# The order of GpSimd's first load and the identity matrix in an attention and gated feed-forward kernel

## The chip, the cores and the metric

The kernel runs on one core of one Trainium2 chip. The metric is the device time of one execution in microseconds (us). Five engines work side by side in a core, each with its own queue of instructions: TensorE (PE in the profile, with PEld for its weight loads), VectorE (DVE), ScalarE (ACT), GpSimd (POOL) and SyncE (SP). DMA transfers are issued from the queues of SP, ACT and POOL, and are carried out by 16 DMA engines.

## The reference

Eight batches of eight heads are read crosswise with a small state, and the result goes through a feed-forward layer with a gate:

```python
def _attn_ref(x, state) -> np.ndarray:          # x (8, 8, 512, 64), state (8, 8, 32, 64)
    scores = scale * np.matmul(x, state.transpose(0, 1, 3, 2))
    ...
    xread = np.matmul(a, state)
    scores2 = scale * np.matmul(state, x.transpose(0, 1, 3, 2))
    ...
    sread = np.matmul(a2, x)
    return np.concatenate([xread, sread], axis=2).astype(np.float32)

def _moe_ref(x, w_gate, w_val, w_out) -> np.ndarray:   # x (4352, 512), d_ff 1536
    gate = np.maximum(x @ w_gate, 0.0)
    val = x @ w_val
    return (gate * val @ w_out).astype(np.float32)
```

The output has 4352 rows of 512 values in float32: for each batch 512 rows from x and 32 from the state.

## The kernel before

The work goes by batch. For each of the eight batches, x is brought in, converted to bf16 (tile xb) and transposed (xT); scores against the transposed state (stT) go to PSUM; ACT takes their exponential (e_sn), and DVE sums and scales it (a_sn), which is transposed once more (ans). Instead of reading the state and then multiplying by the gate and value weights, the kernel first multiplies the state by the weights (tile U, from `u_mm`, L303) and then the attention by U (`gv_mm`, L328). `relu` on ACT and `mult` on DVE make the gated hidden rows (h_sb), and `out_mms` (L365) multiplies them by the output weights. Matmuls of 512 columns at L328 and L365 are most of PE's work.

The order on every engine is written out by hand: `tc.manual_schedule()` at L410 keeps the order in which the instructions are written, and the string `program` (from L456) lists the steps of the first batches one by one, with the PSUM banks that they use. From L492 on, loops go on through the rest. Waits between engines are placed by the framework where data demand them.

What happens at the very start is what the change touches. In the order of the code:

- DVE clears a small tile, `warm` (L411), which PE multiplies by itself (`spin`, L447) while it waits for data. Such spins stand at several places of the program and run whether data are late or not.
- Three loads go out on the hardware queues (L413 to L418): the first pair of heads of batch 0 on SP; on ACT the first part of the state (`state_dma`, L98) and then the second pair of heads. Each pair is 256 KB of float32.
- `make_identity` (masks.py 197 and 199) fills the tile id128, called id in the profile: a memset and an affine select, both on GpSimd. PE uses it as the moving operand of each transpose on PE.
- ACT computes one exponential (L420), so that its table is there.
- DVE sums the identity into a 128 x 2 mask, `odd` (L421), which tells for each partition to which half it belongs. `state_conv` (L122 on ACT) multiplies the state by a column of it.
- GpSimd issues its first load (L427): heads 4 to 7 of batch 0, called the tail (`x_tail`), cast to bf16 on the way into xb, 512 KB of float32.
- The program begins. GpSimd goes on with two such loads for batch 1 (`dx`, L435) and then with the gate and value weights in slices (`dw`, L111), 14 loads in turn, and more after them.

For batch 0, PE's first steps are: the state's transposes (`state_T`, L130), those of the first two pairs of heads (`x_T`, L178), one spin, the scores of these heads (`att_sc`, L209), and then the transposes of the tail (`x_T`, L182), which need the load of L427. The tail's scores, batch 1 (L195), and the first matmuls with the weights (`c_unit`, L303) follow.

Of the kernel before, what the change touches and what calls it, by code (L numbers as in the profile page):

```python
# [12 lines left out]
AX = mybir.AxisListType  # L13
# [3 lines left out]
def kernel(  # L17
# [9 lines left out]
    nc = tc.nc  # L27
# [34 lines left out]
    id128 = const.tile([128, 128], BF16, name="id128")  # L62
# [4 lines left out]
    odd = const.tile([128, 2], FP32, name="odd")  # L67
# [92 lines left out]
    def x_tail(b):  # L160
        return xb[b][:, NC * HK * D:].rearrange("p (h c d) -> p c h d", c=NC, h=HK)
# [251 lines left out]
    for eng, j in ((nc.sync, 0), (nc.scalar, None), (nc.scalar, 1)):  # L413
        if j is None:
            state_dma(eng, 0, 2)
        else:
            src = x[0, 2 * j:2 * j + 2].rearrange("h (p c) d -> p h c d", c=NC)
            eng.dma_start(out=xf[0][:, 2 * j:2 * j + 2], in_=src)  # L418
    make_identity(nc, id128)
    nc.scalar.activation(out=tiny, in_=nc.const_aps.tensor(0.0, (128, 1), FP32), func=AF.Exp)  # L420
    nc.vector.reduce_sum(out=odd, in_=id128.rearrange("p (a h m) -> p h a m", h=2, m=8), axis=AX.XY)  # L421

    def w_load(w, lo, n):
        w_dma((moe_w_gate, moe_w_val)[w], (wg_sb, wv_sb)[w], lo, lo + n)
# [1 line left out]
    xb_alloc(0)  # L426
    nc.gpsimd.dma_start(out=x_tail(0).rearrange("p c h d -> p h c d"),  # L427
                        in_=x[0, HK:H].rearrange("h (p c) d -> p h c d", c=NC))

    def x_load(b, part, parts):  # L430
        if part == 0:
            xb_alloc(b)
            xb[b] = xb[b].rearrange("p (h c d) -> p c h d", h=H, c=NC)
        hs = slice(H * part // parts, H * (part + 1) // parts)
        nc.gpsimd.dma_start(out=xb[b][:, :, hs].rearrange("p c h d -> p h c d"),  # L435
                            in_=x[b, hs].rearrange("h (p c) d -> p h c d", c=NC))
# [154 lines left out]
```

## Time and profile before

| what | us |
|---|---|
| three runs, median (lowest to highest) | 222.43 (221.5 to 223.79) |
| span of the profiled execution, first to last instruction | 219.9 |
| median less that span | 2.5 |
| PE busy in the span | 215.0 |
| DVE busy | 130.3 |
| ACT busy | 124.0 |
| POOL busy | 49.0 |
| DMA: queue of L427, from issue to landing | 6.1 |

For the profiled execution the page gives the span alone; the times of whole executions are those of the three runs. A view of waits gives an engine, the line and tile that waited, what it waited for, and then the sum in us, the number of times and the longest. The chain that ended last is followed back from the last instruction; each of its rows has start, length and what ran. A timeline row has start, length, engine, line, operation, and the tiles written and read. A row of busy time by stretches has the stretch, its length, the busy time of PE, PEld, DVE, ACT and POOL with the number of instructions, the granted clock of PE, the share of the 16 DMA engines that was busy (it can exceed 1 where packets overlap) and GB/s. A row of a DMA queue has packets, MB and the share of the 16 engines' time.

### The profile page before, as it was taken

To read this page: it belongs to the slowest core of one execution; us is meant where nothing else is said; L and a number is where in the kernel's file an instruction comes from. 1 tells how busy PE (TensorE), PEld (TensorE's weight loads), DVE (VectorE), ACT (ScalarE), POOL (GpSimd) and SP (SyncE) were. 2 spreads that over 40 slices of the span, in tenths; PEclk is the share of its full clock that TensorE was granted. 3 is DMA by queue.
4 is the path that set the end of the run, shared out by engine and by line. 5 is a ranking of instruction groups with operands and counts; after the bars stand their busy time and mean duration, and the time that the engine had idled before them with its cause. 6 is when DMAs were issued, how large, how long until landed. Compare 5 with 4: busy or idle time off the path is not lost.

```text
span 219.9 us, 4854 instructions
## 1 busy us (share of the span) xinstructions
PE 215.0 (98%) x1947; PEld 105.1 (48%) x1947; DVE 130.3 (59%) x228; ACT 124.0 (56%) x237; POOL 49.0 (22%) x54
## 2 busy tenths in 40 slices
PE   7899999999999999999999999999999999999994
PEld 3554455444444444444444444445444445666544
DVE  2697898964787569665766487648675333322100
ACT  5599887555667557555566555646654544222222
POOL 8777845360000616015000600000000000000000
PEclk9999999999999999999999999999999999999999
DMA  7999999194048593881358116701411112111132
GB/s 152 176 194 197 197 243 271 64 177 142 22 106 244 102 284 101 136 255 49 96 122 269 52 20 145 118 15 48 105 43 54 49 48 48 52 66 67 57 98 95
DMA packets 41383, 26.27 MB, mean 119 GB/s; under 512 B 22576, under 2 KB 36784, under 8 KB 41360
## 3 DMA queue, kind: packets, MB, share of 16 engines
q1 hardware_dynamic: 28496, 17.73, 31.2%
q0 software_dynamic: 11968, 7.47, 22.1%
q10 hardware_dynamic: 896, 0.75, 1.3%
q8 instruction: 15, 0.25, 0.4%
q14 instruction: 8, 0.07, 0.1%
HBM read 18.35 MB, written 8.91 MB: 124 GB/s over the span
## 4 chain that ended last, share of the span: by engine, by line
PE 94%; DMA 4%; ACT 1%; issue 0%; POOL 0%; DVE 0%; DVEq 0%; POOLq 0%
PE o_ps L365 39%; PE gv_ps L328 38%; PE gv_ps L345 5%; PE up L303 4%; DMA xb<-in_x_dram 3%; PE sc_ps L209 2%; PE upc L303 2%; PE sr_ps L273 1%; PE xT_ps L195 1%; DMA out_dram<-o_sb 1%; PE warm_ps L447 1%; PE aT_ps L244 0%; PE xT_ps L182 0%; ACT o_sb L373 0%; ACT xT L186 0%
## 5 line engine op out<-in xcount | busy, mean ns | idle before, releaser
L365 PE MATMUL o_ps<-wo_sb,h_sb 128*128 128x512 bf16 x372 | 94.6, 379 | 0.0
L328 PE MATMUL gv_ps<-ans,U 128*128 128x512 bf16 x384 | 94.1, 379 | 0.0
L356 DVE TENSOR_TENSOR h_sb<-gv_ps,g_sb 128x512 bf16<-128x512 f32 x96 | 65.2, 689 | 44.7 <-ACT g_sb L352 43.7
L352 ACT ACTIVATE g_sb<-gv_ps 128x512 bf16<-128x512 f32 (+1 forms) x108 | 63.2, 591 | 43.4 <-PE gv_ps L328 32.0
L328 PEld LDWEIGHTS <-U 128*128 128x128 bf16 x384 | 36.3, 98 | 42.2 <-issue 0.6
L365 PEld LDWEIGHTS <-h_sb 128*128 128x128 bf16 x372 | 35.4, 98 | 41.0 <-issue 2.4
L373 ACT COPY o_sb<-o_ps 128x512 f32<-128x512 f32 x31 | 18.3, 590 | 16.5 <-PE o_ps L365 16.5
L313 DVE CAST U<-up 128x512 bf16<-128x512 f32 x36 | 22.7, 684 | 5.0 <-PE up L303 5.0
L313 ACT CAST U<-up 128x512 bf16<-128x512 f32 x36 | 18.9, 594 | 11.7 <-PE up L303 11.7
L151 POOL CAST xb<-xf 128x1024 bf16<-128x1024 f32 x10 | 10.1, 1040 | 65.6 <-DMA xf<-in_x_dram 40.4
L216 ACT ACTIVATE e_sn<-sc_ps 128x512 bf16<-128x512 f32 x16 | 9.6, 599 | 11.1 <-PE sc_ps L209 11.1
L265 POOL COPY xa<-xb 128x2048 bf16<-128x2048 bf16 (+1 forms) x9 | 15.5, 1746 | 1.2 <-POOL xb L151 0.9
L356 DVE TENSOR_TENSOR hs_sb<-gv_ps,g_sb 128x256 bf16<-128x256 f32 x12 | 5.1, 425 | 15.3 <-PE gv_ps L345 10.1
L222 DVE TENSOR_REDUCE cs<-e_sn 128x16 f32<-128x512 bf16 x16 | 10.9, 680 | 4.0 <-ACT e_sn L216 4.0
L228 DVE TENSOR_TENSOR a_sn<-e_sn,rc 128x512 bf16<-128x512 bf16 x16 | 12.6, 793 | 0.4
L323 ACT CAST U<-upc 128x512 bf16<-128x512 f32 (+1 forms) x21 | 10.1, 574 | 0.5 <-PE upc L303 0.4
L303 PEld LDWEIGHTS <-stT 64*32 64x32 bf16 x512 | 5.5, 90 | 9.0 <-issue 7.6
L209 PEld LDWEIGHTS <-xT 128*128 128x128 bf16 x128 | 5.8, 99 | 4.2 <-DVE xT L186 0.8
L303 PE MATMUL up<-wg_sb,stT 64*32 64x512 bf16 x144 | 7.5, 380 | 0.0
L303 PE MATMUL up<-wv_sb,stT 64*32 64x512 bf16 x144 | 7.2, 380 | 0.0
L345 PE MATMUL gv_ps<-br,wg_sb 128*128 128x256 bf16 x48 | 7.2, 273 | 0.0
L345 PE MATMUL gv_ps<-br,wv_sb 128*128 128x256 bf16 x48 | 7.2, 273 | 0.0
(62 smaller groups left out, 116.7 us busy)
## 6 DMA issues: line engine op xcount, KB each, us to landing
out_dram<-o_sb SPq DMA_DIRECT2D x30, 256.0 KB, 2.5
xf<-in_x_dram SPq DMA_DIRECT2D x4, 1024.0 KB, 6.5
wo_sb<-in_moe_w_out_dram POOLq DMA_DIRECT2D x2, 768.0 KB, 13.6
wg_sb<-in_moe_w_gate_dram POOLq DMA_DIRECT2D x5, 256.0 KB, 8.6
wv_sb<-in_moe_w_val_dram POOLq DMA_DIRECT2D x5, 256.0 KB, 9.2
xf<-in_x_dram POOLq DMA_DIRECT2D x1, 1024.0 KB, 15.3
xb<-in_x_dram POOLq DMA_DIRECT2D x3, 256.0 KB, 6.5
xb<-in_x_dram POOLq DMA_DIRECT2D x1, 512.0 KB, 12.0
```

The source lines that it names most:

```text
L209: nc.tensor.matmul(ps[:, :, c, jj], xT[b][:, c, 2 * jp + jj], stT[:, b, 2 * jp + jj], start=True, stop=True)
L222: nc.vector.reduce_sum(out=cs, in_=e_v, axis=AX.X)
L228: {"dve": nc.vector, "pool": nc.gpsimd}[eng].tensor_tensor(out=by_pair(a_sn[b], jp).rearrange("p r (j n) -> p r j n", n=Ns), in0=e_v, in1= ...
L265: nc.gpsimd.tensor_copy(out=v[:, hs:hs + src.shape[1]], in_=src)
L303: nc.tensor.matmul(dst[parity][32 * j:32 * j + 32], stT[r:r + 64, b, j, 32 * parity:32 * parity + 32], wsb[r:r + 64, j, lo:lo + n], start= ...
L313: copy[eng](out=U[b][:, w, kc, lo:lo + 512], in_=held["u", b, w, lo][kc])
L328: nc.tensor.matmul(ps[w], U[b][:, w, kc, f0:f0 + 128], ANS[b][:, kc].rearrange("p c t -> p (c t)"), start=(kc == 0), stop=(kc == NK - 1))
L345: nc.tensor.matmul(ps[w][:, 0:nt], wsb[:, j, f0:f0 + 128], br[:, j].rearrange("p b n -> p (b n)"), start=(j == 0), stop=(j == NJ - 1))
L352: nc.scalar.activation(out=g_sb[:, 0:n], in_=ps[0][:, 0:n], func=AF.Relu)
L356: nc.vector.tensor_tensor(out=dst, in0=ps[1][:, 0:n], in1=held["g", b, jf][:, 0:n], op=ALU.mult)
L365: nc.tensor.matmul(held["o", b, tsub], src[:, jf, tsub * 128:(tsub + 1) * 128], wo_sb[:, jf], start=(jf == 0), stop=(jf == NF - 1))
L373: copy[eng](out=o_sb, in_=held["o", b, tsub])
```

## The change

The identity and the mask are written behind the issue of GpSimd's first load instead of ahead of it. No operation is added or taken away.

```diff
             eng.dma_start(out=xf[0][:, 2 * j:2 * j + 2], in_=src)
-    make_identity(nc, id128)
     nc.scalar.activation(out=tiny, in_=nc.const_aps.tensor(0.0, (128, 1), FP32), func=AF.Exp)
-    nc.vector.reduce_sum(out=odd, in_=id128.rearrange("p (a h m) -> p h a m", h=2, m=8), axis=AX.XY)
 
     def w_load(w, lo, n):
         w_dma((moe_w_gate, moe_w_val)[w], (wg_sb, wv_sb)[w], lo, lo + n)
@@ -426,6 +424,8 @@
     xb_alloc(0)
     nc.gpsimd.dma_start(out=x_tail(0).rearrange("p c h d -> p h c d"),
                         in_=x[0, HK:H].rearrange("h (p c) d -> p h c d", c=NC))
+    make_identity(nc, id128)
+    nc.vector.reduce_sum(out=odd, in_=id128.rearrange("p (a h m) -> p h a m", h=2, m=8), axis=AX.XY)
 
     def x_load(b, part, parts):
```

On GpSimd the issue of L427 comes first, then the memset and the affine select of the identity, then the loads of the program. On DVE the sum keeps its place between the memset of L411 and the cast of the first pair of heads (L155). The queues of SP, ACT and PE have the same instructions in the same order as before.

## The prediction

> **What bounds the kernel now.** I read the page first, for the engine that is full. PE is busy for 215.0 of the 219.9 us of the span, and the granted clock (PEclk) is at 9 tenths or more in every slice.
>
> ```profile
> span 219.9 us, 4854 instructions
> PE 215.0 (98%) x1947; PEld 105.1 (48%) x1947; DVE 130.3 (59%) x228; ACT 124.0 (56%) x237; POOL 49.0 (22%) x54
> ```
>
> So a change of order at the start can only act on the few microseconds in which PE has nothing to do. The view of waits, for PE alone, has just three of them:
>
> ```profile
> PE warm_ps L447 <- DVE hs_sb L411: 1.2, 1, 1.2
> PE xT_ps L182 <- DMA xb<-in_x_dram: 0.6, 1, 0.6
> PE stT_ps L130 <- ACT st_b L122: 0.2, 1, 0.2
> ```
>
> The middle one belongs to the load that is moved. The chain that ended last, in its first 14 us, has the same load as one piece of 6.10 us, with the identity matrix in front of it:
>
> ```profile
> 0.75 0.18 POOL id masks.py:197
> 0.94 0.07 issue
> 1.00 0.29 POOL id masks.py:199
> 1.29 0.14 issue
> 1.43 6.10 DMA xb<-in_x_dram
> 7.52 0.04 issue
> 7.57 0.66 PE xT_ps L182 x16
> ```
>
> The reader is to see that on paper the change takes 0.71 us (1.43 less 0.72, when POOL starts its first own work) off the head of this chain. Then I asked whether the 6.10 us really begin with the issue. The busy time by stretches says what the 16 DMA engines do meanwhile (last two columns: DMA share, GB/s):
>
> ```profile
> 3.25:3.50 0.25, 0.25 (x2) 0.15 (x1) 0.00 (x0) 0.00 (x0) 0.25 (x1) 1.00 1.06 369
> 3.50:3.75 0.25, 0.25 (x2) 0.00 (x0) 0.00 (x0) 0.20 (x1) 0.25 (x1) 1.00 1.12 393
> 3.75:4.00 0.25, 0.25 (x2) 0.00 (x0) 0.00 (x0) 0.25 (x2) 0.25 (x2) 1.00 1.46 283
> 4.00:4.25 0.25, 0.25 (x1) 0.00 (x0) 0.23 (x1) 0.25 (x2) 0.25 (x1) 1.00 0.86 94
> ```
>
> They are full from 2.5 us on, with other loads. The DMA view, cut to short windows, gives packets, MB and share by queue. q0 (software) carries POOL's loads, q1 SP's and q10 ACT's. First 3.50 to 3.75 us, then 3.75 to 4.00, then 4.50 to 5.00:
>
> ```profile
> q10 hardware_dynamic: 94, 0.10, 109.0%
> q1 hardware_dynamic: 3, 0.00, 2.5%
> ...
> q10 hardware_dynamic: 72, 0.06, 73.5%
> q0 software_dynamic: 14, 0.01, 72.4%
> ...
> q0 software_dynamic: 132, 0.07, 130.6%
> ```
>
> The moved load, issued at 1.43, has not one packet before 3.75 us. Its packets begin as ACT's last load (the second x pair) ends: q10 has 94 packets in one quarter of a microsecond, 72 in the next, and 17 from 4.0 to 4.5. The queue of SP has run out just before. So up to about 4 us the load seems to wait for engines, not for its issue.
>
> **The change part by part.**
>
> *The issue, moved ahead.* POOL's rows before are memset 0.72 (0.20 us), affine select 1.00 (0.29), issue 1.43 (0.95), then two x issues from 2.37 (1.50 for both). After: issue at 0.72, done at 1.67. That is 0.71 us earlier. Its length is between 0.75 (half of the 1.50) and 0.95 us. I take 0.95, its own row. It moves past no other DMA issue: SP and ACT start theirs at 0.72 and 1.19 on their own queues, and it stays the first on POOL's.
>
> *The identity, moved back.* It is the same two instructions, now at 1.67 to about 2.24, and 0.95 us later. Its first reader is PE's transpose of the state at 4.51, so 2.27 us of cover remain behind the new end, and the cost is nothing. Counted from the old end (1.29) the cover is 4.51 - 1.29 = 3.22 us; what it is late beyond that goes onto PE's start.
>
> *The mask (DVE reduce, 0.29 us at 1.32).* It follows the identity at about 2.27 and ends at 2.56. On DVE nothing is queued behind it until the x cast at 4.02, which waits 2.41 us for its load. Its reader is ACT's state conversion at 3.54, which waits for the state load. Cover 0.98 us, cost nothing. ACT's own small Exp reads neither and keeps its place.
>
> *The next POOL issues.* Sum of POOL's work unchanged, so the two x issues stay at 2.37 (2.17 if the first took 0.75). The weight issues behind them stay too.
>
> *The landing of the moved load.* This is the whole question, and the trace does not show it directly. Lower bound of the effect on PE: nothing or a loss (below). Upper bound: the load lands 0.71 earlier, 6.82. PE then still has to finish the scores that stand ahead of it, which run from 6.24 to 7.01, so it gains at most 7.57 - 7.01 = 0.56 us. I take zero. The row that decides is the one nearest to the event, q0's empty count until ACT's load thins out, and it says that 1.43 + 2.3 us was not a latency counted from the issue.
>
> *A second gate.* Even a gain at 7.57 has to pass the weights. By the DMA view the second weight load (issued 4.74, 6.9 us) lands at 11.64 and the fourth (issued 6.29, 6.8) at 13.09; PE first uses them here:
>
> ```profile
> 11.78 0.24 PE L303 MATMUL upc<-wv_sb,stT 64*32 64x128 bf16 x8
> ...
> 13.16 0.24 PE L303 MATMUL upc<-wv_sb,stT 64*32 64x128 bf16 x8
> ```
>
> That is 0.14 and 0.07 us of slack. Unless POOL's whole stream moves forward, what PE gains at 7.57 is lost again at 13.1 but for about 0.1 us. The warm-up matmuls between (L447) run in either case. The one thing that can move the stream is its slow start. From 3.75 to 5.00 us q0 has 14 + 66 + 132 = 212 packets; from 6 to 7 it has 353 in 1 us, so 212 are worth 0.60 us and 0.65 us are lost. If that start ran beside the other loads, up to 0.65 us would come back; if not, none.
>
> *The sum*: 0 (identity) + 0 (mask) + 0 (landing), between -0.56 and +1.0 (second rival). The profiled span is 219.9 us, 2.5 below the median of the three runs (222.43); these 2.5 us lie around the span and the change does not touch them. So the forecast stands against the median: 222.4.
>
> *A rule weighed.* The Trainium skill, page "DMA: Bandwidth & Descriptors", section "Latency and other measured facts", gives about 1 us to the first byte of a load issued by GpSimd. By it this load was ready near 2.4 us and then stood behind the others for 1.3 us, so an earlier issue would bring 0. Taken instead as pure latency, the row's 2.3 us would bring the whole 0.71, capped at 0.56. The same page, section "Queues, rings and completion order", says that each engine takes turns between queues, one packet at a time. That speaks against the change, since an earlier load would take turns with the loads of SP and ACT. This trace shows no such turn for q0; it starts where q10 stops.
>
> **The rivals.**
>
> *Faster: the stream really starts earlier.* For it: DMA share is only 0.69 to 0.83 before 2.5 us, so there was room, and the slow start of 0.65 us could lie beside the others. The coincidence of 3.75 us with the end of q10 may be chance. Against it: the engines are full from 2.5 to 4.0 us. Price: tail and weights 0.5 to 0.65 earlier, PE 0.45 to 0.56, so 0.5: 221.9.
>
> *Slower: the moved load takes turns with the second x pair.* PE needs this pair first (cast on ACT at 4.74 when it landed, transposes, scores). From 4.0 to 5.0 us a q0 packet took 100 and then 79 ns (83.1% of 16 engines for 0.5 us over 66 packets, and 130.6% over 132). The pair's 256 packets are 16 to an engine, and one q0 packet before each makes 16 x 0.08 to 0.10 = 1.3 to 1.6 us. PE's pause of 0.56 us swallows the first part. It decides from 0.56 us on, or some 6 or 7 of q0's packets to an engine ahead of the pair's last. Price 1.3 - 0.56 to 1.6 - 0.56, or 0.7 to 1.0: 223.1 to 223.4, taken at 223.1. Against it: at 3.75 us they do not mix. For it: q1 and q10 do both run between 2.15 and 3.5 us.
>
> *Slower by more: the identity comes late.* Affine select after a DMA issue isn't in the trace. It costs from 3.22 us of lateness on and is over 1% from 3.22 + 2.2 = 5.4; taken a little beyond, at 6, PE's start slips by 6 - 3.22 = 2.8 us: 225.2. Nothing in the rows speaks for it; before, it followed the memset within 0.1 us.
>
> **How the numbers follow.** No change 0.42 (222.4, own range 222.1 to 222.7); faster 0.28 (221.9); slower by turns 0.25 (223.1); late identity or another disorder of the start 0.05 (225.2). About 1% (2.2 us) is what a measurement of this kernel can tell from no change, as its three runs lie between 221.5 and 223.79. The first three cases lie inside it. Late identity gives slower 0.05, and I add 0.01 for scatter; faster by over 1% would need more than the three PE pauses hold before 7.57 us (0.56 + 0.16 beside the wait for the first memset), so 0.04 for scatter and what I don't see; the rest, 0.90, is same. The range leaves out the late identity and the outer scatter: the cases reach from 221.9 to 223.4, and with the runs' own half width of about 0.6 to 1 on the side of the gain and less on the other it is 221.2 to 223.8.
>
> **What would show it.** The identity near 1.7 to 2.2 us and the mask ending before 3.5: those steps right. First q0 packets still at 3.75 to 4.0 and PE's first L182 transpose near 7.57: forecast right. First packets near 3.0, L182 near 7.0 to 7.1 and the weights' landings near 11.1 and 12.6: the faster rival. ACT's cast of the second x pair at 5.3 us or later, with scores ending after 7.6: the slower one. I would be wrong altogether if POOL's first issue or affine select had another length than its row, or if PE showed a new wait behind 13 us.

## The result and the profile after

The changed kernel takes 221.27 us (median of 22 runs, 220.9 to 222.65) against 222.47 us for the kernel before (22 runs, 221.42 to 224.53). The ratio is 0.9949, with a 95% interval of 0.993 to 0.9968. Repeated twice with nothing but a comment changed, it was 0.9969 (0.9949 to 0.9989) and 0.9970 (0.9956 to 0.9983). So the change gains 0.3 to 0.5%, some 0.7 to 1.1 us. The forecast was no change, 222.4 us, in a range of 221.2 to 223.8. Four runs that took over 1.5% longer than the fastest of their kernel, two of them about 281 us, are left out of the ratios below.

The two first profiles differ by less than that. The page of the changed kernel:

```profile
span 219.6 us, 4854 instructions
PE 214.8 (98%) x1947; PEld 105.1 (48%) x1947; DVE 129.2 (59%) x228; ACT 124.1 (56%) x237; POOL 49.3 (22%) x54
```

The profiled execution took 221.42 us, 1.8 more than its span. If the same 1.8 lies around the span of 219.9 before, that execution took about 221.7, one of the quick ones of its kernel. One profile of each kernel would therefore have shown only a quarter of the gain.

GpSimd's first microseconds, from the timeline of the changed kernel:

```profile
1.23 0.95 POOL L425 DMA_DIRECT2D xb<-in_x_dram  x1 [0.79 <-POOLq L575]
2.17 0.23 POOL masks.py:197 MEMSET id<- 128x128 bf16 x1
2.48 0.29 POOL masks.py:199 TENSOR_SCALAR_AFFINE_SELECT id<-id 128x128 bf16<-128x128 bf16 x1
2.72 1.50 POOL L435 DMA_DIRECT2D xb<-in_x_dram  x2
```

The reader is to see two things. The issue begins at 1.23 us, not at 0.72 where the memset began before, so it gains 0.20 us and not 0.71. And the second issue moved from 2.37 to 2.72, because the identity now lies between the two.

PE's waits, same view as before the change, in the changed kernel:

```profile
PE warm_ps L447 <- DVE hs_sb L411: 1.2, 1, 1.2
PE stT_ps L130 <- ACT st_b L122: 0.3, 1, 0.3
PE xT_ps L195 <- DMA xb<-in_x_dram: 0.3, 1, 0.3
```

The pause of 0.56 us ahead of the tail's transposes (L182) is gone: they begin at 7.03 instead of 7.57, straight behind the scores. Half of what that gave comes back as a wait for batch 1 (L195), 0.3 us.

The queues of the changed kernel from 3.75 to 4.00 us and then from 4 to 5 us (packets, MB, share of 16 engines):

```profile
q10 hardware_dynamic: 74, 0.07, 81.4%
q0 software_dynamic: 11, 0.01, 17.3%
...
q0 software_dynamic: 255, 0.13, 104.7%
q10 hardware_dynamic: 71, 0.06, 17.9%
```

GpSimd's load starts no earlier than before; it too has its first packets after 3.75 us, while ACT's load is still under way. But once started it runs faster. In the kernel before, the stretch from 4 to 5 us has this:

```profile
q0 software_dynamic: 198, 0.10, 106.9%
q10 hardware_dynamic: 17, 0.01, 3.5%
```

By the DMA view the tail's load now takes 5.8 us from its issue at 1.23 and lands at 7.0; before, it took 6.1 us from 1.43 and landed at 7.5.

Where this ends up is seen at the first use of the second gate's weights. The fourth slice of the value weights (columns 512 to 767, POOL's eleventh load) is first used by PE at these times, in the kernel before and then in the changed one:

```profile
18.70 0.29 PE L303 MATMUL upc<-wv_sb,stT 64*32 64x256 bf16 x8
```

```profile
18.61 0.29 PE L303 MATMUL upc<-wv_sb,stT 64*32 64x256 bf16 x8
```

### The profile page after: what moved, and what is told of

Read it like the earlier page. It is cut to its first block, busy times and chain, and to the rows that moved or that the text cites. A ratio compares the mean times of both kernels' runs of the same rounds, so it can differ in the third digit from the quotient of the medians.

```text
span 219.6 us, 4854 instructions
## 1 busy us (share of the span) xinstructions
PE 214.8 (98%) x1947; PEld 105.1 (48%) x1947; DVE 129.2 (59%) x228; ACT 124.1 (56%) x237; POOL 49.3 (22%) x54
## 4 chain that ended last, share of the span: by engine, by line
PE 93%; DMA 4%; issue 1%; POOL 1%; ACT 0%; DVE 0%; DVEq 0%; POOLq 0%
PE o_ps L365 40%; PE gv_ps L328 38%; PE gv_ps L345 5%; PE up L303 4%; DMA xb<-in_x_dram 3%; PE upc L303 2%; PE sc_ps L209 2%; PE sr_ps L273 1%; DMA out_dram<-o_sb 1%; PE xT_ps L195 1%; PE aT_ps L244 0%; POOL xb L435 0%; PE warm_ps L447 0%; ACT o_sb L373 0%; POOL id masks.py:199 0%
## 5 line engine op out<-in xcount | busy, mean ns | idle before, releaser
L151 POOL CAST xb<-xf 128x1024 bf16<-128x1024 f32 x10 | 10.6, 1086 | 65.5 <-DMA xf<-in_x_dram 47.3
L228 DVE TENSOR_TENSOR a_sn<-e_sn,rc 128x512 bf16<-128x512 bf16 x16 | 11.3, 710 | 0.4
```

The source lines that it names most:

```text
L151: copy[eng](out=xb[b][:, :, hs].rearrange("p c h d -> p h c d"), in_=xf[b][:, hs])
L228: {"dve": nc.vector, "pool": nc.gpsimd}[eng].tensor_tensor(out=by_pair(a_sn[b], jp).rearrange("p r (j n) -> p r j n", n=Ns), in0=e_v, in1= ...
```

## The experiments

Three theories were open. Theory B, my forecast's reason, says that the tail waits for the loads of SP and ACT and not for its own issue. Theory I says that the earlier issue of the tail is what helps, and theory G that it is the gap which the identity now makes between the first and the second issue. Theories A, C and S are explained where they are tested. Ratios are against the kernel before on the same chip, 35 runs of it in each of the three groups; each kernel has 12 runs.

**Both kernels again.** The edit is a comment.

> The kernel before, unchanged but for a comment, for a second profile and for the scatter. Both theories: ratio 1.000 within 0.003. If the pause of PE ahead of the tail's transposes (0.56 us at 7.57) is a fixture of this kernel, it is there again with 0.4 to 0.7 us, and q0's first packets begin again at 3.7 to 3.8 us. If instead the median stands 0.8 us above the first profile because of something that varies from run to run, this profile shows another place where PE lost time.

> The changed kernel, unchanged but for a comment, for a second profile. Both theories: ratio near 0.995, no pause at the tail's transposes, GpSimd's first issue at 1.2 us again and not at 0.7.

Measured: 0.9992 (0.9972 to 1.0012) and 0.9969 (0.9949 to 0.9989). The second profiles are far apart. Before, with PE's first use of the same slice, then the changed kernel's PE waits up to 40 us:

```profile
19.49 0.30 PE L303 MATMUL upc<-wv_sb,stT 64*32 64x256 bf16 x8
```

```profile
PE warm_ps L447 <- DVE hs_sb L411: 1.2, 1, 1.2
PE stT_ps L130 <- ACT st_b L122: 0.3, 1, 0.3
PE sc_ps L209 <- DVE xT L186: 0.2, 1, 0.2
```

No load is in the latter list. PE used the slice at 17.90. So the median of the kernel before stands above its first profile because of something that differs from run to run, and this something is over by 19 us.

**The cost doubled.**

```diff
     make_identity(nc, id128)
+    make_identity(nc, id128)
```

> The kernel before with the identity built twice ahead of GpSimd's first issue: the cost that the change takes away is doubled (issue near 2.0 us instead of 1.43). Theory A (the tail's landing follows its issue): landing some 0.3 to 0.6 us later, PE's pause grows from 0.56 to 0.9 or more, time 222.9 to 223.2, ratio 1.002 to 1.004. Theory B (my forecast's reason: the tail waits for the other loads, not for its issue): q0's first packets still at 3.75 us, landing and pause as before, ratio 1.000. Theory C (PE's pause costs through the clock alone): as A only if the pause grows.

Measured: 0.9999 (0.9981 to 1.0018), as B has it and A has not. GpSimd's timeline:

```profile
1.63 0.29 POOL masks.py:199 TENSOR_SCALAR_AFFINE_SELECT id<-id 128x128 bf16<-128x128 bf16 x1
1.98 0.95 POOL L428 DMA_DIRECT2D xb<-in_x_dram  x1
2.93 1.51 POOL L436 DMA_DIRECT2D xb<-in_x_dram  x2
```

An issue 0.55 us later cost nothing that these runs show. Contrary to both theories, the tail's transposes even began earlier, at 7.04 with a wait of 0.2 us.

**PE's pause filled.**

```diff
-ex.0.0 xT.0.2@0
+ex.0.0 spin.2 xT.0.2@0
```

> The kernel before with two more warm-up matmuls (0.43 us of PE work) in PE's pause ahead of the tail's transposes; the loads are as before. Theory A (the gain is the earlier landing): no gain, ratio 1.000 to 1.001, since PE still waits for the same landing. Theory C (PE's pause costs more than its length, because the clock is granted later or is lost in some runs): the median falls towards the changed kernel's, ratio 0.995 to 0.998, and the scatter of the runs shrinks.

Measured: 0.9990 (0.9970 to 1.0009). C falls for the median, at least at its full size. Its other half, that fewer runs lose the clock, is left open: the mean granted clock was 0.998 or more in all 11 runs that count, and 0.992 or less in 9 of the 35 of the kernel before. PE's waits up to 40 us:

```profile
PE upc L303 <- DMA wv_sb<-in_moe_w_val_dram: 0.2, 1, 0.2
PE xT_ps L182 <- DMA xb<-in_x_dram: 0.2, 1, 0.2
```

0.43 us of idle work in the pause was free, and a wait for the value weights appears. The pause was not what set the median.

**Less work for PE ahead of the weights.**

```diff
-spin.2 c.0.0.128@30
+c.0.0.128@30
...
-spin.1 c.0.128.128@25
+c.0.128.128@25
```

> The kernel before without three of the warm-up matmuls (two ahead of the first matmuls with the weights, one ahead of the second lot), 0.65 us of PE work less between 11.2 and 13.1 us. Theory S (the second gate: PE waits for the weight slices whatever it did before): waits of PE for the weights appear, the time is unchanged, ratio 0.999 to 1.001. Rival (PE's own work sets the pace there): 0.4 to 0.65 us less, ratio 0.997 to 0.998.

Measured: 1.0006 (0.9984 to 1.0028). Up to 40 us PE waits among others for:

```profile
PE xT_ps L182 <- DMA xb<-in_x_dram: 0.6, 1, 0.6
PE upc L303 <- DMA wv_sb<-in_moe_w_val_dram: 0.3, 1, 0.3
```

0.65 us less work did not move the median, and half of it shows up as a wait for the value weights. In this profile theory S holds: at this place the stream of weights sets the pace. The ratio shows it less well. The mean granted clock was 0.992 or less in 5 of the 12 runs, against 6 of 35 of the kernel before; the median of the other 7 is 221.76 us, against 222.22 for the other 29, and 7 runs don't decide whether this is a gain.

**Early issue and gap, each alone.** In the first kernel below an unused identity (tile id2) is built behind the tail's issue, with the real one ahead of it as before; in the second the identity and the mask follow the second issue.

```diff
                         in_=x[0, HK:H].rearrange("h (p c) d -> p h c d", c=NC))
+    make_identity(nc, id2)
```

> The kernel before with a second, unused identity built between GpSimd's first and second issue: first issue at 1.43 as before, second at 2.9 instead of 2.37. Theory G (gap): q0's first 2.5 us carry 280 to 340 KB instead of 200 to 250, the tail lands at 7.0 or earlier, ratio 0.995 to 0.998. Theory I (issue): nothing gained, later weights if anything, ratio 1.000 to 1.002.

```diff
-    dx.1.0.2 dx.1.1.2 stc.0.0.act
+    dx.1.0.2 id dx.1.1.2 stc.0.0.act
```

> GpSimd's first issue ahead of all as in the changed kernel, but the identity and the mask only behind the second issue: first issue at 1.23, second at 2.18 without a gap, mask ready near 3.7, which costs the state's conversion 0.1 to 0.2 us that PE's pause can swallow. Theory I: gain as in the changed kernel or a little more, since the second issue is earlier as well, ratio 0.993 to 0.997. Theory G: no gain, ratio 1.000 to 1.001.

Measured: gap alone 0.9980 (0.9965 to 0.9994), early issue alone 0.9986 (0.9964 to 1.0008). GpSimd's timeline, gap alone and then early issue alone:

```profile
1.43 0.95 POOL L428 DMA_DIRECT2D xb<-in_x_dram  x1
...
2.92 1.51 POOL L437 DMA_DIRECT2D xb<-in_x_dram  x2
```

```profile
1.22 0.95 POOL L425 DMA_DIRECT2D xb<-in_x_dram  x1 [0.79 <-POOLq L577]
2.17 0.76 POOL L433 DMA_DIRECT2D xb<-in_x_dram  x1
```

Both were built as meant. Each lies between the two kernels. The interval of the gap alone ends below the 1.000 that theory I expects, so the gap by itself gains something. That of the early issue alone overlaps with both theories, and this kernel has a cost of its own: its mask comes late, and PE waited 0.5 us for the state's conversion (L130) where it had waited 0.2. The traces say more (table below).

**Half of the identity ahead.** The memset stays in front, the affine select follows the issue.

> The identity cut in two: its memset stays ahead of GpSimd's first issue, its affine select follows. Theory I (the issue's time counts): GpSimd's first issue stood still until 1.23 us in the changed kernel though the engine was free at 0.6, so it starts at 1.23 here too, and the gain is that of the changed kernel, ratio 0.995 to 0.997. Theory G (it is the gap of 0.55 us between the first and the second issue that counts): the gap falls to about 0.3 us, second issue near 2.45, and so does the gain, ratio 0.997 to 0.999.

Measured: 0.9988 (0.9965 to 1.0011), with the second issue at 2.55. The ratio decides nothing. The profiled execution took 224.45 us. PE's longest wait in it, and the clock (the column behind POOL's) from 7.25 to 14 us:

```profile
PE xT_ps L182 <- DMA xb<-in_x_dram: 1.7, 1, 1.7
...
7.25:14.00 6.75, 5.32 (x65) 3.67 (x67) 3.09 (x7) 2.23 (x4) 4.82 (x7) 0.50 1.54 175
```

The tail came late (8.35 us), PE stood idle for 1.7 us ahead of it, and the granted clock then fell to half. Its q0 had 266 packets from 4 to 5 us, with the issue at 1.26.

**Without the second pair's load.**

```diff
-    for eng, j in ((nc.sync, 0), (nc.scalar, None), (nc.scalar, 1)):
+    for eng, j in ((nc.sync, 0), (nc.scalar, None)):
```

> The kernel before without ACT's load of the second pair of heads (256 KB); the cast reads the first pair again, so the scores of heads 2 and 3 are computed from heads 0 and 1. GpSimd's first issue stays at 1.43 us. Theory B (q0 starts where the loads of SP and ACT end): q0's first packets at 3.0 to 3.2 us instead of 3.75 to 3.9, tail, second weight slice and all behind 0.5 to 0.7 us earlier, ratio 0.997. Theory L (the 2.3 us are the delay of GpSimd's path from the issue): first packets still at 3.7 to 3.9, and of the time only what the missing traffic saves on the way, ratio 0.999 to 1.000.

The issue stood at 1.41. The queues from 3.25 to 3.50 us and from 3.50 to 3.75:

```profile
q1 hardware_dynamic: 39, 0.03, 38.4%
q0 software_dynamic: 11, 0.01, 16.9%
...
q0 software_dynamic: 30, 0.02, 83.2%
q1 hardware_dynamic: 6, 0.00, 4.1%
```

With the pair gone, q0 begins as SP's load runs out, half a microsecond earlier than in any kernel with the pair. Theory B on the start is shown. The time was 0.9990 (0.9963 to 1.0016), which holds the forecasts of both theories: the earlier start then ran slowly, with 209 packets from 4 to 5 us. The tail's transposes began at 7.05, yet the fourth value slice was used at 18.72, as in the kernel before (18.70).

**Once more, and a wider gap.** In the last two the memset of the ones column (step `on`) is moved ahead of the second issue, in the changed kernel and in the kernel before.

> The changed kernel for the third time, beside the two that follow. Issue at 1.23, gap 0.55 us: ratio 0.995 to 0.997. Theory I (early issue) and theory G (gap) both expect this; if each brings a part, this one stands below early issue alone (0.9986) and gap alone (0.998).

> The changed kernel with the memset of the ones column (0.42 us on GpSimd, now among the weight issues) moved between GpSimd's first and second issue as well: issue at 1.23, gap near 1.0 us, second issue near 3.1. Theory G: at least the gain of the changed kernel, ratio 0.993 to 0.996, the tail landing at 7.0 or earlier. Theory I: as the changed kernel, 0.995 to 0.997. Rival: the later second issue starves nothing, but if it does, batch 1 lands later and the ratio rises to 0.998 or more.

> The kernel before with that memset moved between GpSimd's first and second issue: issue at 1.43 as before, gap near 0.45 us, no work added. Theory G: as the unused identity at the same place, ratio 0.997 to 0.999. Theory I: no gain, 0.999 to 1.001, and q0's first 1.2 us as slow as before (under 120 KB by 5 us from the start).

Measured: 0.9970 (0.9956 to 0.9983), 0.9970 (0.9943 to 0.9998) and 1.0007 (0.9985 to 1.0030). The wider gap was not built. GpSimd's timeline of the second of these kernels:

```profile
2.72 0.38 POOL L451 MEMSET xa<- 128x64 bf16 x1
2.81 1.50 POOL L435 DMA_DIRECT2D xb<-in_x_dram  x2
```

The memset lasts 0.38 us but the next issue begins 0.09 us into it, so it made a gap of only 0.09 us more. The two kernels are thus copies of the changed kernel and of the kernel before, and count as such, though the profile of the second copy was taken while the clock was lost (below). No version beat the changed kernel.

**The traces side by side.** Times in us; packets are q0's from 4 to 5 us; "tail" is the start of PE's transposes of it; "slice" is PE's first use of the fourth value slice; "rest" is the time of the profiled execution less "slice".

| kernel | 1st issue | 2nd issue | packets | tail | slice | rest |
|---|---|---|---|---|---|---|
| before | 1.43 | 2.37 | 198 | 7.57 | 18.70 | |
| before again | 1.43 | 2.38 | 130 | 7.60 | 19.49 | 202.80 |
| pause filled | 1.42 | 2.37 | 183 | 7.53 | 19.41 | 202.82 |
| fewer spins | 1.43 | 2.37 | 165 | 7.52 | 18.95 | 202.79 |
| late, memset between | 1.43 | 2.46 | 210 | 8.16 | 20.40 | 202.84 |
| identity twice | 1.98 | 2.93 | 175 | 7.04 | 18.89 | 202.81 |
| gap alone | 1.43 | 2.92 | 183 | 7.13 | 18.86 | 202.86 |
| early issue alone | 1.22 | 2.17 | 285 | 7.79 | 18.93 | 202.94 |
| changed | 1.23 | 2.72 | 255 | 7.03 | 18.61 | 202.81 |
| changed again | 1.23 | 2.73 | 331 | 6.75 | 17.90 | 202.82 |
| changed, third | 1.23 | 2.73 | 304 | 7.03 | 18.16 | 202.79 |
| early, memset between | 1.23 | 2.81 | 302 | 7.07 | 18.27 | 202.87 |

Three things are to be read. First, "rest" is the same within 0.15 us in all of them while "slice" runs over 2.5 us: what one execution gains or loses against another is decided before PE reaches this slice, and little behind it adds or takes away. Second, the packets fall into two groups that don't touch: 130 to 210 where the identity stands ahead of the first issue, 255 to 331 where the issue stands ahead of the identity's select. But the packets don't rank the slices: the early issue alone has 285 and uses its slice at 18.93, later than the kernel before with 198 (18.70). Third, the tail begins at 7.13 or before wherever the second issue is at 2.72 or later, and at 7.52 or later wherever it is at 2.46 or before.

The latest slice, 20.40 in the copy of the kernel before, has a second cause, the clock: by the DMA view its load had landed at 19.5, and PE came to it 0.9 us later. PE's wait for the tail there, and the stretches around it:

```profile
PE xT_ps L182 <- DMA xb<-in_x_dram: 1.4, 1, 1.4
...
4.50:7.90 3.40, 1.64 (x21) 1.09 (x21) 1.21 (x4) 1.24 (x3) 3.31 (x5) 1.00 1.22 137
7.90:11.30 3.40, 3.14 (x42) 2.33 (x42) 1.98 (x5) 1.18 (x2) 1.55 (x3) 0.50 1.56 173
```

This and the half identity's are the only two profiles of the fourteen in which the clock is seen to fall ahead of the last microseconds, and the only two with a pause of over 0.7 us ahead of the tail. The run list tells how often it happens. The mean granted clock was 0.992 or less in 23 of 105 runs of the kernel before, and in 3 of 58 of the changed kernel with its copies. So part of the gain may be that the clock is lost less often. That part is the smaller one: among the runs above 0.992 the changed kernel and its copies in the experiments have medians of 221.25, 221.54 and 221.42, the kernel before beside them 222.00 and twice 221.99, which is still a gain of 0.2 to 0.3%.

## Why the prediction was right or wrong

*That PE is full but for its start, and the change can act only there*: right. It holds more strictly than I wrote ("rest"). The clock, full in every slice of the page that I read, is part of that start: in two later profiles it fell to 0.50 there.

*The issue gains 0.71 us*: wrong, 0.20. The row from which I took 0.72 is that of a memset; a first load issue was not shown at that time in any row, and it begins at 1.22 or 1.23 in every kernel that has it first. I should have put down 0 to 0.71 for it.

*The tail waits for engines, not for its issue*: right for the start of the stream. Doubling the delay cost nothing, and taking ACT's load away moved the start. But "it starts where q10 stops" was read too sharply: from 3.75 to 4.50 us both queues had packets, 72 and then 17 of ACT's beside 14 and then 66 of GpSimd's.

*The landing, zero*: this is the step that failed. The tail landed 0.5 us earlier, at 7.0 instead of 7.5, close to my upper bound. I took the start of the stream for the whole of it. I had put the slow start at 0.65 us, saw that it could come back only "if that start ran beside the other loads", and there stopped. It came back otherwise: the stream starts at the same time and is quicker in its first microsecond. Between 4 and 5 us there are 178 packets on the average of the seven kernels above with the identity ahead, and 295 in the five others, 117 more. At the 353 in 1 us that I read from 6 to 7 us, that is 0.33 us, an estimate. It isn't shown that these packets make the gain, since the early issue alone had 285 of them and gained less. That 221.27 still lies in the range was luck: it is below the 222.1 to 222.7 of the forecast itself, and 0.07 us inside an end that was set for the scatter of the runs.

*The second gate*: right, and as far as the traces go it is the one that counts. I used it to argue that a gain at PE's pause would be lost again, and so it was in the changed kernel: 0.54 us ahead at the tail, 0.10 at 13.06, 0.09 at 18.61. Filling the pause or taking out spins did not move the median. The time goes with the first use of the slices, and in the three profiles of the changed kernel the fourth value slice is used at 18.22 us on the average, in the two of the kernel before at 19.10: 0.87 us, about the gain measured, though single profiles of one kernel differ by as much as 0.8.

*The second issue stays at 2.37*: wrong, 2.72. It did no harm that shows, goes with the earlier tail, and gained 0.2% when it was made alone.

*Identity and mask at no cost*: right, with less cover than I had. The mask ended at 3.10; ACT's conversion at 3.66 waited for the state's load.

*The 2.5 us around the span*: wrong; it is 1.8, and 0.7 was the scatter of the runs.

*The rivals.* "Faster" had the direction right and, at 0.5 us, a price below the 0.7 to 1.1 measured, but its own sign in the trace, first packets near 3.0, did not come. "Slower by turns" fell by its price and its sign: ACT's cast of the second pair began at 4.92 instead of 4.74 us, short of the 5.3 that I had named. The two loads did run side by side, with 71 packets of ACT's and 255 of GpSimd's from 4 to 5 us.

The cause of the gain is thus located, ahead of the fourth value slice, but not shown. What stays open: why the stream starts quicker when the issue stands ahead of the identity. It isn't simply the earlier time, since an issue at 1.98 started no worse than one at 1.43 (175 packets against 130 to 210). Order against the affine select and a threshold between 1.26 and 1.42 us would both fit. Open too is how much of the gain belongs to the early issue and how much to the later second one: alone they gave 0.14% and 0.20%, together 0.3 to 0.5%, with intervals that allow much. And open is how much of it is a clock that is lost less often.

## What to carry to other kernels

When loads overlap from the start, ask when the stream behind the first load is up to speed, and not only when its first packet goes: a kernel that is fed by one stream for its first 20 us keeps whatever that stream gains or loses. Find the last gate that depends on the stream and subtract it from the time; if the rest is constant over several profiles, what differs between runs lies ahead of the gate, in the stream or, as in two profiles here, in a long pause and the clock that is lost behind it. Read the granted clock of every run before you compare medians. And where single runs scatter by 1%, one profile of each kernel doesn't show a gain of 0.5%; take several of each before you explain.

## What the runs showed of the hardware

- GpSimd's first load issue begins at 1.22 to 1.26 us where nothing or one memset stands ahead of it, while a memset at the same place begins at 0.72.
- A GpSimd load that is issued at 1.23, 1.43 or 1.98 us has its first packets after 3.75 us in each case, while the last packets of ACT's hardware load still run; without that load they come between 3.25 and 3.50.
- A small GpSimd memset (128x64, 0.38 us) runs beside the next load issue, which begins 0.09 us after it, while memset and affine select of the identity hold the next issue back by 0.55 us.
- In the two profiles where PE stood idle for 1.4 and 1.7 us ahead of the tail, the granted clock fell to 0.50, for 3.4 us and for 6.8 us. In the twelve others that pause was at most 0.7 us and no such fall is seen.
- The first microsecond of the stream varies from run to run: 130 and 198 packets from 4 to 5 us in two profiles of the kernel before, 255 to 331 in three of the changed one.
